# A fused attention and MLP kernel: seven block products for eight in the last blocks of the first MLP product, one more batch turned by DMA, new priorities

## The chip, the core and the metric

The kernel runs on one core of a Trainium2 chip. The metric is the device time in microseconds (us) of one execution; three executions of the kernel before took 311.2, 312.96 and 313.85 us, and their median, **312.96 us**, is the time before. Besides that one execution was profiled; its span from the first to the last instruction is 311.4 us, and all times "at" which something happens are counted from the start of that span.

TensorE (PE in the profile) multiplies matrices into PSUM, a memory of eight banks of 512 fp32 columns for each of 128 partitions. ScalarE (ACT), VectorE (DVE) and GpSimd (POOL) work on tiles; SyncE (SP) issues transfers. Each engine takes its own instructions strictly in order and waits on semaphores for the others.

## What is computed

The reference, cut to what matters:

```python
# 8 batches, 8 heads, 576 tokens, 64 per head; omega: 128 x 64
scale = 1.0 / np.sqrt(np.sqrt(D))
def phi(x):                                   # x = q*scale or k*scale
    proj = np.einsum('bhsd,md->bhsm', x, omega)
    sq = np.sum(x * x, axis=-1, keepdims=True) / 2.0
    h = proj - sq
    h = h - np.max(h, axis=-1, keepdims=True)
    return np.exp(h) / np.sqrt(m)
q_p, k_p = phi(q_s), phi(k_s)
kv = np.einsum('bhsm,bhsd->bhmd', k_p, v)
z = np.sum(k_p, axis=2)
num = np.einsum('bhsm,bhmd->bhsd', q_p, kv)
den = np.einsum('bhsm,bhm->bhs', q_p, z)[..., None] + 1e-06
attn = num / den
x = attn.transpose(0, 2, 1, 3).reshape(4608, 512)
h = x @ w_in                                  # first MLP product, 512 -> 2048
g = h * np.clip(h + 3.0, 0.0, 6.0) / 6.0
out = g @ w_out                               # second MLP product, 2048 -> 512
```

So a linear attention over features gives x (4608 tokens of 512), and a two-layer MLP with the hard-swish function follows.

## The kernel before

The kernel is written as a list of operations with what each reads and writes, its possible engines, its expected duration and a priority. A list scheduler in the kernel's own Python code (class Prog) sorts these into one fixed order for each engine, gives PSUM banks to the operations' results ("Virt" is a bank that is asked for), and puts in the semaphore waits. A table NUDGE shifts single priorities and changes nothing but the order.

The tokens are worked on in nine blocks of 512: blocks 0 to 7 are the first 512 tokens of each batch, block 8 the 64 left over of each batch. While TensorE does the MLP of one block it also does the attention of a later batch, so matmuls of several kinds lie between each other. The first MLP product of a block is made by feature columns, 16 groups of 128:

```python
    def mm1(blk, f):
        ...
        def e(E):
            for c in range(NJ):                                  # NJ = 4 pieces of the 512 inputs
                ins = E.matmul(ring.t[vh.slot], wi[:, c, 128 * f:128 * f + 128], xv[:, c, :],
                               start=(c == 0), stop=(c == NJ - 1))
            return ins
        op("PE", 4 * mmt(512), e, t, ..., name="mm1.%d.%d" % (blk, f))            # L998
        op("ACT", ..., lambda E: E.activation(tsb[tu][:], ring.t[vh.slot], AF.Relu,
                                              bias=0.5, scale=1.0 / 6.0), ...)     # L1004
        op("DVE", ..., lambda E: E.scalar_tensor_tensor(gT[gu][:, f, :], tsb[tu][:], 1.0,
                                              ring.t[vh.slot], ALU.min, ALU.mult), ...)  # L1006
```

The second MLP product (L1132) already goes by seven products of quarters in place of eight from block 1 on. GpSimd makes the sums of quarters of g that it needs (L1064); VectorE adds its parts (L1148). Block 0's first and second product are at L1023 and L1048, the very last product at L1198.

```python
    def products(blk):
        h0, ha, hb = Virt(ring), Virt(ring), Virt(ring)          # three PSUM banks
        plan = [(h0, 0, block(blk, 0, 0), B11, ...), (h0, 0, block(blk, 0, 1), B21, ...),
                (ha, 0, S2[gu], T2, ...), (ha, 0, S3[gu], B12, ...), (hb, 0, block(blk, 1, 0), T1, ...),
                (ha, 0, block(blk, 1, 1), T4, ...), (hb, 0, block(blk, 0, 1), B22, ...)]
        # each: 16 matmuls of 256 columns
```

Attention turns q, k and its own output x by 128 x 128 pieces. The first three batches (0 to 2) are turned on TensorE (L511) with a copy out of PSUM behind it; from the fourth batch on a transposing DMA does it:

```python
    PE_T, PE_X = 3, 3          # batches below this number: q/k and x turned on TensorE
        ...
        if b < PE_X:
            turn_x(0, 4, [0, 1])
        else:
            op("SP", 0.9, lambda E: E.dma_start_transpose(
                xT[pb][:, m, :].rearrange("p (t k) -> p t k", t=4), xm[pb][:, m, :]), ...)   # L974
```

From the fourth batch on (ROWS = 3) the projections of k and q come in "bursts" of matmuls over 64 rows, two at a time on the two halves of the array (L736 and L739). k and q of successive batches land in two buffers in turn (one of them is the memory of the fp32 staging of batch 0), and so does x:

```python
    half = k32[:].rearrange("p c d -> p (c d)").bitcast(BF16)
    KB = [kb, half[:, 0:NCH * D]...]                  # k of even / odd batches
    QB = [qb, half[:, NCH * D:2 * NCH * D]...]
    xb = [sbt("xb%d" % u, [128, XW], BF16) for u in range(2)]
```

Before the first inputs have landed, TensorE is given filler matmuls (L548) that compute nothing of use.

Of the kernel before, what the change touches and what calls it, by code (L numbers as in the profile page):

```python
# [15 lines left out]
ROWS = 3  # L16
# [6 lines left out]
    ('Tevk0.00', 0): 0.0222, ('Tk0.10', 0): 0.0169, ('Tevk0.10', 0): 0.0216, ('Tk0.11', 0): 0.0313,  # L23
    ('Tevk0.11', 0): 0.0172, ('castq0.0A', 0): -0.0176, ('Tevq0.1A', 0): 0.1639, ('Tq0.1B', 0): -0.0037,
    ('Tevq0.1B', 0): 0.3021, ('Tk0.l', 0): 0.4022, ('Tevk0.l', 0): 0.0235, ('K0.0', 0): -0.1553,
    ('eK0.0', 0): -0.0153, ('K0.1', 0): 0.0442, ('eK0.1', 0): -0.0653, ('mx0.1', 0): -0.0395, ('eK0.2', 0): -0.042,
    ('K0.3', 0): 0.0766, ('K0.4', 0): 0.1229, ('eK0.4', 0): 0.2718, ('K0.5', 0): -0.0067, ('eK0.5', 0): 0.0177,
    ('K0.6', 0): -0.0736, ('eK0.6', 0): 0.1839, ('mx0.6', 0): 0.3237, ('K0.7', 0): -0.0092, ('eK0.7', 0): 0.8775,
    ('K0.8', 0): 0.0351, ('eK0.8', 0): 0.0218, ('mx0.8', 0): -0.0031, ('eQ0.0A', 1): 0.7881, ('vcl.0', 1): 0.0286,
    ('cc.0.0', 0): 0.1338, ('kvz.0.0', 0): 0.1537, ('num.0.0A', 0): 0.0042, ('rec.0.0A', 0): -0.0049,  # L30
    ('div.0.0A', 0): 0.0356, ('num.0.0B', 0): 0.0126, ('vc.0.1', 0): 0.4124, ('kv.0.1', 0): -0.0134,
    ('kvz.0.1', 0): 0.8635, ('num.0.1A', 0): 0.0126, ('rec.0.1A', 0): -0.009, ('div.0.1A', 0): 0.177,
    ('Xev.0.1A', 0): 0.6709, ('num.0.1B', 0): -0.0007, ('cc.0.2', 0): -0.0088, ('vc.0.2', 0): 0.1154,
    ('vcc.0.2', 0): -0.0808, ('num.0.2A', 0): 0.0126, ('rec.0.2A', 0): 0.08, ('vc.0.3', 0): -0.0114,
    ('vcc.0.3', 0): -0.0172, ('num.0.3A', 0): 0.7836, ('X.0.3B', 0): 0.0821, ('Xev.0.3B', 0): 0.0062,
    ('numL0', 0): -0.0033, ('divL0', 0): 0.0082, ('divL2', 0): 0.0082, ('k00.1', 0): 0.0095, ('kl.1', 0): -0.0088,
    ('ql0.1', 0): 0.0145, ('vl.1', 0): -0.119, ('v10.1', 0): -0.0099, ('Tevq1.2', 0): 0.0463, ('Tq1.4', 0): 0.7514,
    ('mx1.4', 0): -0.179, ('eK1.5', 0): 0.3592, ('mx1.5', 0): 0.3227, ('eK1.6', 0): 0.7632, ('mx1.7', 0): -0.561,
    ('mx1.8', 0): 0.0033, ('Q1.0', 1): 0.0073, ('eQ1.0', 1): 1.061, ('Q1.1', 0): 0.0184, ('Q1.1', 1): -0.0218,
    ('eQ1.1', 1): 0.9399, ('Q1.2', 1): 0.3729, ('eQ1.2', 1): -0.007, ('Q1.3', 0): 1.0729, ('vcl.1', 1): -0.0035,  # L40
    ('cc.1.0', 0): -0.1361, ('vc.1.0', 0): 0.0089, ('kv.1.0', 0): 0.0071, ('kvz.1.0', 0): -0.0003,
    ('rec.1.0A', 0): 0.0024, ('div.1.0A', 0): 0.0054, ('div.1.0B', 0): 0.0054, ('vc.1.1', 0): 0.0087,
    ('num.1.1A', 0): -0.002, ('div.1.1A', 0): 0.0054, ('div.1.1B', 0): 0.0054, ('Xev.1.1', 0): -0.0002,
    ('kv.1.2', 0): 0.9899, ('rec.1.2A', 0): -0.0101, ('div.1.2A', 0): 0.0075, ('div.1.2B', 0): 0.0054,
    ('X.1.2', 0): 0.0047, ('vc.1.3', 0): 0.6341, ('rec.1.3A', 0): -0.0016, ('div.1.3A', 0): 0.0054,
    ('div.1.3B', 0): 0.0054, ('mm1.0A.0p', 2): 0.0169, ('mm1.0A.2p', 1): 0.003, ('mm1.0A.2p', 2): 0.026,
    ('mm1.0A.4p', 2): 0.0282, ('mm1.0A.4', 0): 0.0113, ('relu.0A.4', 0): 0.1116, ('mm1.0A.6', 0): -0.0758,
    ('relu.0A.6', 0): -0.0575, ('mm1.0A.8', 0): -0.0075, ('g.0A.8', 0): -0.037, ('g.0A.10', 0): 0.0321,
    ('relu.0A.12', 0): 0.0317, ('mm1.0A.14', 0): 0.0222, ('relu.0B.12', 0): 0.7429, ('relu.0B.14', 0): 0.6881,
    ('k10.2', 0): -0.0002, ('kl.2', 0): -0.7114, ('q10.2', 0): 0.511, ('ql0.2', 0): 0.6465, ('Tevq2.3', 0): -0.6541,  # L50
    ('Tq2.4', 0): 1.2316, ('K2.2', 0): -0.7584, ('K2.5', 0): -0.3285, ('mx2.5', 0): -0.1483, ('K2.6', 0): 0.784,
    ('K2.7', 0): -0.0504, ('K2.8', 0): -0.1148, ('mm2.0.0', 3): -0.0049, ('mm2.0.0', 5): 1.9062,
    ('mm2.0.0', 6): 0.0051, ('mm2.0.1', 2): 0.0111, ('mm2.0.1', 5): 0.4836, ('mm2.0.2', 0): -0.0003,
    ('mm1.1.0', 0): -1.129, ('mm1.1.8', 0): -1.8251, ('g.1.8', 0): 0.0106, ('mm1.1.1', 0): -1.2275,
    ('mm1.1.9', 0): -0.9344, ('relu.1.9', 0): 0.0261, ('mm1.1.2', 0): -0.5674, ('mm1.1.10', 0): -1.3861,
    ('mm1.1.11', 0): -0.0435, ('mm1.1.4', 0): -0.3428, ('mm1.1.12', 0): 0.0488, ('mm1.1.13', 0): -0.1387,
    ('relu.1.13', 0): -0.4107, ('mm1.1.14', 0): 0.8048, ('mm1.1.7', 0): 0.8803, ('relu.1.7', 0): 0.0128,
    ('g.1.7', 0): -0.0389, ('mm1.1.15', 0): 1.161, ('k10.3', 0): -0.0369, ('kl.3', 0): 0.0052, ('q00.3', 0): -0.0024,
    ('q10.3', 0): 0.0694, ('ql0.3', 0): -0.0408, ('ql1.3', 0): -0.013, ('eK3.3.0', 0): 1.4387, ('R3.4', 0): -0.4628,
    ('eQ3.4', 0): -0.8607, ('kv.3.1', 0): 1.0065, ('vcc.3.2', 0): -0.4962, ('kv.3.2', 0): 0.1102,  # L60
    ('cc.3.3', 0): -0.8518, ('kvz.3.3', 0): 0.0243, ('P1.2', 0): 0.9757, ('P1.4', 0): 0.3487, ('P1.5', 1): -0.0512,
    ('P1.6', 1): 0.5369, ('mm1.2.0', 0): -1.4622, ('mm1.2.8', 0): -1.4018, ('mm1.2.1', 0): -1.442,
    ('g.2.1', 0): -0.019, ('mm1.2.9', 0): -0.3004, ('mm1.2.2', 0): -0.8136, ('mm1.2.11', 0): 0.359,
    ('mm1.2.12', 0): 0.5284, ('mm1.2.5', 0): 0.5493, ('mm1.2.6', 0): 0.5785, ('mm1.2.14', 0): 0.4337,
    ('mm1.2.7', 0): 0.6223, ('mm1.2.15', 0): 0.272, ('kl.4', 0): 1.3248, ('q00.4', 0): 3.3283, ('R4.4', 0): 1.7005,
    ('kv.4.1', 0): 1.244, ('kv.4.2', 0): 2.3155, ('rec.4.2B', 0): -0.9675, ('rec.4.3B', 0): -2.0089,
    ('P2.0', 0): 0.8372, ('mm1.3.2', 0): 0.2569, ('mm1.3.3', 0): 1.5479, ('mm1.3.4', 0): 1.276,
    ('mm1.3.5', 0): 1.2524, ('mm1.3.13', 0): 1.3245, ('mm1.3.6', 0): 1.4395, ('relu.3.6', 0): -0.4435,
    ('mm1.3.14', 0): 1.2483, ('mm1.3.7', 0): 1.5772, ('relu.3.7', 0): -0.3792, ('mm1.3.15', 0): 2.2545,
    ('kl.5', 0): 1.5071, ('q00.5', 0): -1.2639, ('eQ5.1', 0): -0.7262, ('eK5.2.0', 0): -1.0927,  # L70
    ('eK5.2.1', 0): -0.7425, ('eQ5.2', 0): -0.2778, ('eQ5.2', 1): -1.2134, ('eK5.3.0', 0): -1.1241,
    ('eQ5.3', 0): -0.7781, ('eQ5.3', 1): -1.1002, ('rec.5.0B', 0): 0.3333, ('num.5.1A', 0): 0.9799,
    ('vc.5.2', 0): -0.2083, ('div.5.2A', 0): 1.0671, ('P3.0', 0): 1.894, ('p1.3', 0): -2.2681,
    ('mm1.4.8', 0): -0.5145, ('mm1.4.1', 0): -1.527, ('S24.0', 0): 0.3404, ('relu.4.10', 0): -0.4615,
    ('mm1.4.11', 0): 0.2614, ('g.4.11', 0): 1.1488, ('S24.3', 0): -0.7607, ('eK6.0.0', 0): 1.1035,
    ('R6.1', 0): -0.8985, ('eQ6.1', 0): 1.5979, ('vc.6.0', 0): -1.609, ('vcc.6.0', 0): -1.6609, ('kv.6.0', 0): 0.7643,
    ('S44.1', 0): -1.9992, ('P4.2', 1): -0.8623, ('P4.3', 1): -2.077, ('P4.4', 1): -1.4771, ('mm1.5.0', 0): -1.6247,
    ('mm1.5.8', 0): -0.9391, ('mm1.5.1', 0): -1.9248, ('S35.0', 0): 0.1833, ('mm1.5.2', 0): -1.0023,
    ('relu.5.2', 0): 1.3127, ('mm1.5.11', 0): -1.1438, ('mm1.5.6', 0): 0.544, ('mm1.5.14', 0): 0.9483,
    ('mm1.5.7', 0): 0.6794, ('k00.7', 0): -0.8986, ('k10.7', 0): -1.1588, ('kl.7', 0): -0.7342, ('q10.7', 0): -0.2825,  # L80
    ('ql0.7', 0): -1.5109, ('ql1.7', 0): -1.5993, ('R7.1', 0): -1.3631, ('eQ7.1', 1): -0.9517, ('R7.4', 0): -0.7767,
    ('kv.7.0', 0): -0.5374, ('num.7.0A', 0): -0.5449, ('div.7.2B', 0): 1.8188, ('kv.7.3', 0): 0.8011,
    ('kvz.7.3', 0): 2.1121, ('num.7.3A', 0): 0.8703, ('P5.0', 0): 0.8394, ('P5.4', 0): 0.6698,
    ('mm1.6.0', 0): -0.9734, ('mm1.6.8', 0): -0.5602, ('mm1.6.1', 0): -0.5771, ('mm1.6.9', 0): -0.2962,
    ('mm1.6.2', 0): -0.4166, ('mm1.6.10', 0): -0.1926, ('mm1.6.3', 0): -0.3888, ('mm1.6.11', 0): 0.3862,
    ('mm1.6.12', 0): 0.4482, ('mm1.6.13', 0): 0.606, ('mm1.6.6', 0): 0.5263, ('mm1.6.14', 0): 0.7093,
    ('mm1.6.15', 0): 0.6324, ('P6.0', 0): 0.8219, ('P6.2', 0): 0.2249, ('P6.2', 1): -0.859, ('P6.4', 0): 0.6817,
    ('P6.6', 0): -0.9586, ('P6.6', 1): -1.2152, ('mm1.7.7', 0): -1.7654, ('P7.5', 1): 0.9958, ('P7.6', 1): 0.9926,
# [1225 lines left out]
```

The softmax here doesn't subtract the row's maximum and nothing guards it: scores larger than these inputs give would overflow.

## Time and profile before

| | |
|---|---|
| time, median of three | 312.96 us |
| span of the profiled execution | 311.4 us |
| TensorE busy | 301.0 us (97%) |
| VectorE busy | 231.9 us (74%) |
| GpSimd busy | 230.2 us (74%) |
| ScalarE busy | 195.5 us (63%) |
| moved by DMA | 43.17 MB, mean 139 GB/s |

How to read it. A page of the profile gives for each engine the time in which it was busy and its share of the span, then the same in 40 equal slices as tenths. PEld is the loading of weights into the array, which overlaps the matmuls. The "chain that ended last" is followed back from the last instruction, at each step to what released it. A "group" is all instructions of one line, engine and operation: busy time and mean duration of one in ns, then the idle time of the engine just before them and what ended it. Matmul durations contain their passage through the array and so overlap; the pace of a row of matmuls is its length divided by their number. The same holds, to a lesser degree, of the other engines. The other views used are the busy time by stretch, the timeline, and the chain in order of time (start, length, engine and line, number).

### The profile page before, as it was taken

The page shows a single profiled execution, that of the slowest core. Times are in us where ns is not written, and L with a number is a line of the kernel's source. Part 1 is how long each engine was busy: PE and PEld are TensorE (multiplying, and loading weights), DVE is VectorE, ACT ScalarE, POOL GpSimd, SP SyncE. Part 2 cuts the span into 40 slices and gives each one's busy share as a digit, 9 for nine tenths or more (in the row PEclk, how much of TensorE's full clock was granted, in tenths as well). Part 3 has the DMA queues.
Part 4 walks back from the last instruction along what each step waited for, and adds up shares of the span by engine and source line. Part 5 has one row for each costly group of instructions (what it writes and reads, how often), then busy time and mean ns, then how long its engine had stood idle before and what let it go on. Part 6 is the DMA issues. An engine that isn't in the chain of part 4 may idle for free.

```text
span 311.4 us, 7144 instructions
## 1 busy us (share of the span) xinstructions
PE 301.0 (97%) x2723; PEld 204.4 (66%) x2750; DVE 231.9 (74%) x511; ACT 195.5 (63%) x448; POOL 230.2 (74%) x246
## 2 busy tenths in 40 slices
PE   7999999999999999999999999998999999999993
PEld 5679966555775578656864685467745864567783
DVE  4898998797778965879687977975978627558543
ACT  3786898598658763878389836992867106455200
POOL 2687454299989797499959995999759936839990
PEclk9999999999999999999999999999999999999999
DMA  7999999997747899389959992999511201010036
GB/s 240 254 205 182 249 180 161 255 113 100 158 131 98 96 251 221 141 111 153 252 129 168 199 179 85 127 188 213 133 78 37 42 10 61 2 67 0 2 135 137
DMA packets 83218, 43.17 MB, mean 139 GB/s; under 512 B 51056, under 2 KB 80880, under 8 KB 83184
## 3 DMA queue, kind: packets, MB, share of 16 engines
q1 hardware_dynamic: 55824, 29.60, 40.4%
q0 software_dynamic: 26576, 12.46, 32.3%
q10 hardware_dynamic: 784, 0.66, 0.7%
q8 instruction: 22, 0.36, 0.5%
q14 instruction: 12, 0.10, 0.1%
HBM read 36.73 MB, written 9.44 MB: 148 GB/s over the span
## 4 chain that ended last, share of the span: by engine, by line
PE 80%; POOL 8%; ACT 3%; DMA 2%; issue 2%; DVE 2%; SPq 1%; POOLq 0%; DVEq 0%
PE p L998 30%; PE p L1132 27%; PE p L1048 5%; PE p L1023 4%; POOL s L1064 4%; PE p L929 2%; DMA q<-in_q_dram 2%; PE p L511 2%; PE p L900 2%; PE p L736 2%; POOL gT L1064 1%; POOL vc L884 1%; PE p L739 1%; PE p L771 1%; PE p L788 1%
## 5 line engine op out<-in xcount | busy, mean ns | idle before, releaser
L1006 DVE SCALAR_TENSOR_TENSOR gT<-tsb,p 128x512 f16<-128x512 f16 x128 | 84.9, 681 | 28.4 <-ACT tsb L1004 27.7
L1004 ACT ACTIVATE tsb<-p 128x512 f16<-128x512 f32 x128 | 74.8, 600 | 45.1 <-PE p L998 36.7
L998 PE MATMUL p<-xT,wi 128*128 128x512 bf16 x427 | 101.2, 379 | 1.5 <-issue 0.3
L998 PEld LDWEIGHTS p<-xT,wi 128*128 128x128 bf16 x448 | 42.2, 98 | 44.0 <-issue 1.1
L1132 PE MATMUL p<-wo,gT 128*128 128x256 f16 x368 | 45.7, 273 | 0.0
L1064 POOL TENSOR_TENSOR s<-gT 128x512 f16<-128x512 f16 x32 | 37.0, 1156 | 11.8 <-DVE gT L1006 9.8
L1064 POOL TENSOR_TENSOR s<-gT,s 128x512 f16<-128x512 f16 x32 | 37.0, 1156 | 8.8 <-DVE gT L1006 6.7
L1064 POOL TENSOR_TENSOR gT<-gT,s 128x512 f16<-128x512 f16 x32 | 36.9, 1153 | 5.7 <-PE p L1132 3.4
L1132 PEld LDWEIGHTS p<-wo,gT 128*128 128x128 f16 x368 | 35.0, 98 | 6.8 <-issue 0.8
L1064 POOL TENSOR_TENSOR gT<-gT 128x512 f16<-128x512 f16 x32 | 37.4, 1167 | 2.4
L749 ACT ACTIVATE kp<-p 128x512 bf16<-128x512 f32 (+1 forms) x50 | 25.8, 560 | 19.4 <-PE p L739 19.3
L754 DVE TENSOR_REDUCE mx<-kp 128x4 f32<-128x512 bf16 (+1 forms) x50 | 29.6, 625 | 4.5 <-ACT kp L749 4.0
L1132 PE MATMUL p<-t,gT 128*128 128x256 f16 x256 | 32.1, 273 | 0.0
L945 DVE TENSOR_TENSOR xb<-p,rec 128x384 bf16<-128x384 f32 (+1 forms) x64 | 28.5, 476 | 0.2
L884 POOL TENSOR_TENSOR vc<-v,cc 128x512 bf16<-128x512 f32 x22 | 23.4, 1062 | 6.9 <-DVE cc L878 4.9
L758 ACT ACTIVATE qpT<-p 128x512 bf16<-128x512 f32 (+1 forms) x50 | 26.5, 576 | 2.2 <-PE p L739 2.2
L1132 PEld LDWEIGHTS p<-t,gT 128*128 128x128 f16 x256 | 24.2, 98 | 5.6 <-issue 1.2
L1148 DVE TENSOR_TENSOR u<-p 128x512 f32<-128x512 f32 x16 | 11.0, 690 | 13.4 <-PE p L1132 13.4
L780 DVE TENSOR_REDUCE mx<-kp 128x4 f32<-128x512 bf16 x27 | 17.5, 675 | 1.2 <-ACT kp L777 1.2
L886 ACT ACTIVATE vc<-v,cc 128x64 bf16<-128x64 f32 x72 | 18.2, 351 | 0.0
L811 POOL TENSOR_TENSOR vcl<-vl,cc 64x260 bf16<-64x260 f32 x14 | 8.7, 620 | 11.8 <-DVE cc L807 11.0
L929 PEld LDWEIGHTS p<-kvz,qpT 128*128 128x128 bf16 x312 | 14.2, 98 | 4.9 <-ACT qpT L792 0.5
(101 smaller groups left out, 474.6 us busy)
## 6 DMA issues: line engine op xcount, KB each, us to landing
v<-in_v_dram SPq DMA_DIRECT2D x14, 512.0 KB, 5.1
out_dram<-osb SPq DMA_DIRECT2D x14, 512.0 KB, 2.7
wi<-in_moe_w_in_dram POOLq DMA_DIRECT2D x4, 512.0 KB, 9.0
k<-in_k_dram POOLq DMA_DIRECT2D x8, 256.0 KB, 4.6
k<-in_q_dram POOLq DMA_DIRECT2D x8, 256.0 KB, 5.3
wo<-in_moe_w_out_dram POOLq DMA_DIRECT2D x8, 256.0 KB, 12.3
kb<-in_k_dram POOLq DMA_DIRECT2D x6, 256.0 KB, 5.1
qb<-in_q_dram POOLq DMA_DIRECT2D x6, 256.0 KB, 5.2
```

The lines of the kernel that those rows point to most:

```text
L749: op("ACT", actt(128 * n), lambda E, lh=lh, ko=ko: E.activation(ko, out_of(0, lh).rearrange("p (x m) -> p x m", m=M), AF.Exp, scale=alpha) ...
L754: op("DVE", dvet(128 * n), lambda E, ko=ko, mo=mo: E.reduce_max(mo, ko, axis=AX.X), pos(u) + 0.03, reads=[("kp", 0, u + lh) if i else ("kp ...
L758: op("ACT", actt(128 * n), lambda E, lh=lh: E.activation(qd[:, d0:d1, lh, :], out_of(1, lh).rearrange("m (j t) -> m j t", t=128), AF.Exp, ...
L884: return E.tensor_tensor(vcm[:, :, 0:D], v32[:, m, :, :], cbc, ALU.mult)
L886: ins = E.activation(vcm[:, i, 0:D], v32[:, m, i, :], AF.Copy, scale=cc[pb][:, c0 + i:c0 + i + 1])
L929: ins = E.matmul(d[:, hh, i - i0, :], qpT[pb][:, o:o + 128], kvz[m][:, 65 * hh:65 * hh + 65], start=True, stop=True)
L945: op("DVE", dvet(128 * n), lambda E: E.tensor_tensor(xv(i0, i1), psum()[:, :, :, 0:64], rbc, ALU.mult), t + 0.01, reads=[vn, ("rec", ru)], ...
L998: ins = E.matmul(ring.t[vh.slot], wi[:, c, 128 * f:128 * f + 128], xv[:, c, :], start=(c == 0), stop=(c == NJ - 1))
L1004: op("ACT", actt(512), lambda E: E.activation(tsb[tu][:], ring.t[vh.slot], AF.Relu, bias=0.5, scale=1.0 / 6.0), t - 0.1, reads=[vh], write ...
L1006: op("DVE", dvet(512), lambda E: E.scalar_tensor_tensor(gT[gu][:, f, :], tsb[tu][:], 1.0, ring.t[vh.slot], ALU.min, ALU.mult), t - 0.1, re ...
L1064: op(engines, {"POOL": 0.05 + n / 490.0, "DVE": 0.07 + n / 1920.0}, lambda E: E.tensor_tensor(dst, x, y, ALU.subtract if minus else ALU.ad ...
L1132: ins = E.matmul(ring.t[v.slot][:, 256 * j:256 * j + 256], a[:, f, 128 * j:128 * j + 128], w[:, f, :], start=(first and f == 0 and j == 0) ...
```

## The change: what it does and what it is for

1. **Seven products for eight in the first MLP product**, for the second half of block 7's feature groups and all of block 8. A pair of feature groups (f and f + 8) and the two halves of the tokens and of the inputs make 2 x 2 quarters. Sums of quarters of w_in (input_sums, once, on VectorE) and of x (x_sums, for both blocks, on VectorE or GpSimd) take the place of some quarters. Seven products of quarters, each of two matmuls of 256 columns, replace eight. The parts are put together in PSUM: TensorE adds to a bank, ScalarE copies from bank to bank, VectorE adds. It is meant to take matmul time away.

2. **Third batch's output turned by transfers**: PE_X goes from 3 to 2, so batch 2's x is turned by DMA rather than on TensorE.

3. **Types and buffers.** x and w_in are held in f16 in place of bf16. The memory of the fp32 staging of batch 0 now holds the sums, so that k and q have one buffer for all batches, and so has x.

4. **Bursts.** Their code is rewritten, with a list of ranges (BURSTS) of the same five ranges; it applies from the same batch on. Their order among the rest comes from other priorities, and the batches from the fifth on have a shorter step (APACE).

5. **Priorities**: a new NUDGE table, and another expected duration of GpSimd's sums in the scheduler.

The diff, cut to its core (cuts marked with ...):

```diff
 NUDGE = {
-    ('Tevk0.00', 0): 0.0222, ...
+    ('k00.0', 0): -0.0886, ...
@@
+    ROWS = 3
+    BURSTS = [[(0, 2)], [(2, 6)], [(6, 10)], [(10, 14)], [(14, 18)]]
+    FAST = 4
+    APACE = 0.06
-    PE_T, PE_X = 3, 3
+    PE_T, PE_X = 3, 2
@@
-    half = k32[:].rearrange("p c d -> p (c d)").bitcast(BF16)
-    KB = [kb, half[:, 0:NCH * D]...]
-    QB = [qb, half[:, NCH * D:2 * NCH * D]...]
+    stage = [t[:].rearrange("p c d -> p (c d)").bitcast(F16) for t in (k32, q32)]
+    W2s, W3s = [stage[0][:, 2048 * i:2048 * i + 2048]... for i in range(2)]
+    W4s = stage[1][:, 0:2048]...
+    X1s, X2s, X4s = ...                       # further parts of stage
-    xb = [sbt("xb%d" % u, [128, XW], BF16) for u in range(2)]
-    xT = [sbt("xT%d" % u, [128, NJ, MAIN], BF16) for u in range(2)]
-    wi = sbt("wi", [128, NJ, DFF], BF16)
+    xb = [sbt("xb", [128, XW], F16)] * 2
+    p7 = [sbt("p7_%d" % u, [128, 256], F32) for u in range(2)]
+    X3s = [sbt("x3_%d" % u, [128, 2, 256], F16) for u in range(2)]
+    xT = [sbt("xT%d" % u, [128, NJ, MAIN], F16) for u in range(2)]
+    wi = sbt("wi", [128, NJ, DFF], F16)
@@
+    FIRST7 = (8, 7)          # first block of feature groups 0-3 and 4-7
+    AHEAD = 2                # a pair starts when the pair two before has ended
+    def input_sums(h):       # W1..W4 of 128x1024 each, on VectorE
+        ...
+    def x_sums(blk):         # X1..X4 of 128x512 each, on VectorE or GpSimd
+        ...
+    def mm1_pair(blk, f):
+        U, V = Virt(ring, True), Virt(ring, True, True)          # two PSUM banks
+        ...
+        def e_a(E):
+            two(E, half(U, 0), orig(0, 0), b[0][0], True)        # two matmuls of 256 columns
+            return two(E, half(U, 1), summed(W3s), X3s[u])
+        def e_b(E):
+            two(E, half(V, 1), summed(W2s), X2s[u])
+            return two(E, half(U, 0), orig(0, 1), b[1][0])
+        def e_d(E):
+            two(E, half(V, 1), orig(1, 1), X4s[u])
+            return two(E, half(V, 0), summed(W4s), b[1][1])
+        op("PE", 2 * each, e_a, ..., name="mm1a." + nm)
+        op("ACT", actt(256), lambda E: E.copy(half(V, 1), half(U, 0)), ..., name="s1." + nm)
+        op("ACT", actt(256), lambda E: E.copy(p7[w7][:], half(U, 1)), ..., name="s3." + nm)
+        op("PE", 2 * each, e_b, ..., name="mm1b." + nm)
+        op("ACT", actt(256), lambda E: E.copy(half(V, 0), half(V, 1)), ..., name="s2." + nm)
+        op("PE", each, lambda E: two(E, half(V, 0), summed(wi[:, 0:2, 1024:2048]), X1s[u]), ..., name="mm1c." + nm)
+        op("DVE", dvet(256), lambda E: E.tensor_tensor(half(U, 1), half(V, 0), p7[w7][:], ALU.add), ..., name="a2." + nm)
+        op("DVE", dvet(256), lambda E: E.tensor_tensor(half(V, 1), half(V, 1), p7[w7][:], ALU.add), ..., name="a1." + nm)
+        op("PE", 2 * each, e_d, ..., name="mm1d." + nm)
+        # then Relu on ScalarE and min-and-multiply on VectorE for U and V, 512 columns each, as before
@@
-        op(engines, {"POOL": 0.05 + n / 490.0, ...
+        op(engines, {"POOL": 0.07 + n / 455.0, ...
```

In the pair the order is fixed by what each piece reads: a, then the copies s1 and s3, then b, then the copy s2, then c, then the additions a2 and a1, then d.

## The prediction

> **What bounds the kernel now.** I read the page first (shares of engines, the slices), then the chain that ended last, then busy time by stretch, then the groups. The page:
>
> ```profile
> PE 301.0 (97%) x2723; PEld 204.4 (66%) x2750; DVE 231.9 (74%) x511; ACT 195.5 (63%) x448; POOL 230.2 (74%) x246
> PE   7999999999999999999999999998999999999993
> PEclk9999999999999999999999999999999999999999
> PE 80%; POOL 8%; ACT 3%; DMA 2%; issue 2%; DVE 2%; SPq 1%; POOLq 0%; DVEq 0%
> ```
>
> TensorE (PE) is busy in every slice but the first and the last, at the full clock, and 80% of the chain that ended last is its own. The stretches say where the rest is:
>
> ```profile
> core 0: us, PE busy (x) PEld busy (x) DVE busy (x) ACT busy (x) POOL busy (x), PEclk, DMA share, GB/s
> 0.00:22.00 22.00, 19.31 (x200) 13.62 (x201) 15.53 (x51) 14.50 (x32) 11.90 (x22) 1.00 1.00 235
> 191.00:225.00 34.00, 33.00 (x315) 21.64 (x317) 26.09 (x60) 25.57 (x64) 29.57 (x32) 1.00 0.85 158
> 253.00:276.00 23.00, 22.89 (x130) 12.72 (x130) 14.11 (x21) 11.34 (x20) 11.87 (x11) 1.00 0.12 47
> 276.00:292.00 16.00, 15.90 (x112) 10.98 (x113) 10.07 (x17) 7.80 (x14) 13.66 (x13) 1.00 0.01 1
> 292.00:311.40 19.40, 14.52 (x141) 12.80 (x138) 8.19 (x14) 0.33 (x1) 11.34 (x10) 0.96 0.38 109
> ```
>
> From 22 us to 306 us TensorE hardly pauses: even the worst stretch, 191 to 225, lacks 1.0 us. In the last two blocks (253 to 292) it lacks 0.2 us of 39. Up to 22 us the program waits for its first inputs, and part of PE's busy time there is filler (59 matmuls at L548). So past the start the time is TensorE's work laid end to end, and a change is worth the matmul time that it takes away, less the waits that it brings in. From the chain in order of time I take the pace of each kind:
>
> ```profile
> 39.83 0.67 PE p L511 x12
> 280.30 2.59 PE p L998 x12
> 291.59 13.17 PE p L1132 x120
> ```
>
> A 128-column transpose costs 0.67/12 = 0.056 us, a 512-column matmul of the first product 2.59/12 = 0.216 us, a 256-column one 13.17/120 = 0.110 us. The mean durations in the groups (379 and 273 ns) are longer because they overlap. Two 256-column matmuls cost 0.22 us, the same as one of 512, so cutting the product into quarters costs nothing by itself.
>
> **What the Trainium skill says.** "TensorE: Matmul & The Clock Gate", section "Back-to-back issue gap", gives an isolated gap of N/2.4 + 2.5 ns when warm: 216 ns for 512 columns, 109 for 256, 56 for 128. The trace agrees with all three; the 131 ns that the same section gives for sustained streams of 512 is not seen here. "VectorE: DVE Perf Modes", section "Why PSUM operands drop a tier", says that fp32 PSUM operands hold VectorE to its 1x mode; the trace agrees, 681 to 692 ns for 512 elements, so each added 256-column addition in PSUM will be near the 416 ns of the 128x256 group below. "DMA: Bandwidth & Descriptors", section "DMA Transpose (X-bar)", says that a transposing DMA takes 2-byte types only; xb goes from bf16 to f16, which is still 2 bytes, so the transfers should keep their median landing time of 4.0 us.
>
> **The change part by part.**
>
> ```profile
> L1006 DVE SCALAR_TENSOR_TENSOR gT<-tsb,p 128x512 f16<-128x512 f16 x128 | 84.9, 681 | 28.4 <-ACT tsb L1004 27.7
> L1004 ACT ACTIVATE tsb<-p 128x512 f16<-128x512 f32 x128 | 74.8, 600 | 45.1 <-PE p L998 36.7
> L499 ACT COPY xT<-p 128x256 bf16<-128x256 bf16 x5 | 1.8, 374 | 0.9 <-PE p L511 0.9
> L865 DVE TENSOR_TENSOR xb<-p,rec 128x256 bf16<-128x256 f32 x2 | 0.8, 416 | 0.0
> L511 PE MATMUL p<-ident,xb 128*128 128x128 bf16 x48 | 5.3, 219 | 0.1
> ```
>
> *Seven products for eight.* Half of block 7 and all of block 8, 24 of the 144 feature columns of 128, go over to pairs: 12 pairs. A pair took 8 matmuls of 512 columns, 8 x 0.216 = 1.73 us; it now takes 14 of 256, 14 x 0.1095 = 1.53 us. The instruction orders of both programs agree: 512 matmuls of 512 columns become 416, and 168 of 256 columns come in. TensorE saves 96 x 0.216 - 168 x 0.1095 = 20.7 - 18.4 = **2.3 us**, all in the stretch where it had no idle time.
>
> What it costs elsewhere: per pair three ScalarE copies of 128x256 (374 ns each in the group above) and two VectorE additions of 128x256 (416 ns). Over 12 pairs ScalarE gets 36 x 0.374 = 13.5 us more and VectorE 24 x 0.416 = 10.0 us more. In 253 to 292 they had 11.34 + 7.80 = 19.1 us and 14.11 + 10.07 = 24.2 us of 39. ScalarE goes to 32.6 us, VectorE to 34.2 us, plus six of the eight sums of x quarters on it (some 0.35 us each, estimated from half of the 0.67 us that a 1024-element f16 sum took: 2.1 us), 36.3 us in all. The stretch itself shrinks to 36.7. That looks full, but durations count overlap: where operations follow each other without a wait, VectorE starts a 512-element one every 0.60 us, not 0.69 (3 in 2.05 us at 274 us in the timeline), and ScalarE one every 0.48. By pace VectorE has some 31 of 36.7. The eight weight sums (8 x some 0.7 = 5.6 us of VectorE) lie mostly (six of the eight, by the order) before block 7's pairs, where VectorE had 20.1 of the 28 us from 225 to 253.
>
> *The round trips.* Inside a pair TensorE waits three times for another engine. After a group comes the drain, 273 - 109 = 0.16 us, and some 0.03 us of signalling (ScalarE ends at 256.70, VectorE starts at 256.73). So: a 0.44, out 0.19, copy 0.40, b 0.44, out 0.19, copy 0.40, c 0.22, out 0.19, two additions 0.77, d 0.44: a chain of 3.7 us for 1.53 us of TensorE. Alone it would stall more than half of the time. But the new order puts 208 matmuls of the second product (22.8 us) between the pieces, and lets two pairs run at once: TensorE has (18.4 + 22.8)/12 = 3.4 us of work per pair, 6.9 us for two, against a chain of 3.7. So most pieces find their operand waiting. Where two copies or a Relu stand ahead of the one needed, a piece is late by a few tenths. I put **0.7 us** for all 12 pairs; this is a choice.
>
> *Third batch's output by transfers.* The 48 transposes of xb become 32; 16 x 0.056 = **0.9 us** off TensorE, and the copies out of PSUM with them (four of 512 columns). Four more DMA transposes at 4.0 us land well ahead: in that stretch the second block's products run and DMA is not full.
>
> *Buffers.* The batches' k and q now land in one pair of buffers instead of two (the old second pair holds the sums), and xb is single. A load must wait until the previous batch has been turned. A batch has some 32 us; landing takes 5 us and the turns 4 us each. **0** expected.
>
> *Priorities and bursts.* The same 180 + 50 matmuls of the bursts; five vc scalings move from GpSimd to ScalarE. TensorE idles so little between 22 and 292 that better priorities can give back about 1 us at most. In the start, 60 filler matmuls for 59 say that the scheduler expects the same empty time. I take **-0.3 us**.
>
> Sum: 312.96 - 2.3 - 0.9 + 0.7 - 0.3 = 310.2. As the list of priorities was made for this order, and such lists are kept where they help, I go a little lower: **309.8 us**, 1.0% less.
>
> **The rivals.** (1) *The round trips eat the gain.* Engines take their work in order, so one late copy delays the matmuls behind it, those of the second product too. For it: three waits per pair, ScalarE and VectorE both near nine tenths by duration, and two PSUM banks held per pair beside three of the second product, of eight. Against it: 6.9 us of work over a 3.7 us chain. At 0.3 us per wait, 36 waits are 10.8 us and the change would be slower, near 320; at 0.1 us they are 3.6 and the change is worth nothing. (2) *VectorE becomes the bound of the last two blocks*: if it really takes 0.69 us for each operation, 36.3 us of 36.7 leaves no room and some 2 us are lost: 311.5. (3) *The single buffers delay a batch*: a burst late by 2 us is covered as long as other matmuls are ready; only if the block before had run out would it cost, 1 to 3 us. (4) *The priorities do more than I see*, above all in the first 22 us: with an earlier first product 2 us less, 307.8.
>
> **Range and chances.** The three runs before span 311.2 to 313.85, so the measure alone wanders by a per cent. Sums of the good cases (no late pieces, 1 us from priorities, 1 us from the start) give 307.5; of the bad (rivals 1 and 2 at 0.1 us a wait) 313. Range 306.8 to 312.8. Faster by over 2% means under 306.7, which needs rival 4 whole and nothing lost: 0.09. Slower by over 2% means over 319.2, rival 1 in full: 0.03. Within 2%: 0.88.
>
> **What the profile after will show.** If right: TensorE's matmul time down by 3.2 us; PE still near nine tenths or more in every slice from the third to the last but one; in the last two blocks, waits of PE for ScalarE copies and VectorE additions that sum to under 1.5 us; VectorE and ScalarE at 80 to 90% there; first product at L1023's successor starting near 21.5 us as before. The saving is wrong if 256-column matmuls at odd weights run slower than 0.1095 us; the 0.7 is wrong if the pieces of pairs show gaps of 0.2 us or more each; the buffers are wrong if TensorE idles between 92 and 253 us by clearly more than the 2.3 us of 161 that it lacks there now by the same view of stretches. Wrong altogether if the last stretch grows rather than shrinks.

## The result, and the profile after

The changed kernel takes **308.59 us** (median of six executions, 308.26 to 310.21), the kernel before beside it 311.92 us (six, 310.85 to 313.85): a ratio of 0.9896, with a 95% interval of 0.9856 to 0.9936. The profiled execution of the kernel after spans 306.5 us. Its page, first the shares of the engines, then two rows of slices and the shares of the chain that ended last:

```profile
PE 298.6 (97%) x2804; PEld 210.0 (69%) x2807; DVE 246.1 (80%) x543; ACT 215.4 (70%) x522; POOL 229.9 (75%) x248
...
PE   8999999999999999999999999999999899999994
...
PE 88%; DVE 4%; ACT 3%; DMA 2%; SPq 2%; issue 1%; DVEq 0%
```

TensorE is still busy throughout, and its part of the chain grew from 80% to 88%. GpSimd left the chain, in which it had 8%; VectorE has 4% where it had 2%. The busy time by stretch of the kernel after, cut where its blocks 7 and 8 lie (start:end, length, busy time of PE, PEld, DVE, ACT, POOL):

```profile
0.00:22.00 22.00, 20.19 (x220) 15.44 (x221) 16.05 (x54) 15.44 (x35) 13.33 (x23) 1.00 1.06 247
...
225.00:241.20 16.20, 14.97 (x118) 7.96 (x114) 15.71 (x33) 7.48 (x16) 8.00 (x7) 1.00 0.29 70
241.20:253.00 11.80, 11.80 (x85) 8.15 (x86) 10.17 (x20) 8.32 (x19) 10.50 (x9) 1.00 0.01 1
253.00:276.00 23.00, 23.00 (x204) 19.56 (x202) 18.49 (x34) 14.67 (x34) 21.05 (x19) 1.00 0.12 47
276.00:289.00 13.00, 13.00 (x122) 11.63 (x120) 11.45 (x22) 8.29 (x19) 12.11 (x11) 1.00 0.01 2
```

From 241.2 to 289 us, where the twelve pairs lie but for the first piece of the first one (at 239.4 us), this view shows no idle time of TensorE: the round trips cost nothing that it can see. The one lack is just ahead of them, 1.2 us between 225 and 241.2, and there VectorE is full (15.71 of 16.2). The list of TensorE's waits in the kernel after, from 18 us on (who waits, for whom, us in all, times, longest), has only two entries:

```profile
PE p L1037 <- DVE gT L1045: 1.2, 1, 1.2
PE p L1037 <- ACT qpT L832: 0.5, 1, 0.5
```

What VectorE did ahead of the first is told by its chain in order of time (start, length, engine and line):

```profile
232.83 0.81 DVE xb L984 x2
234.15 0.68 DVE gT L1045
234.83 1.34 DVE q L1222
236.17 0.87 DVE gT L1045 x2
237.28 1.50 DVE wi L1222
238.78 1.30 DVE q L1222
240.53 0.61 DVE gT L1045
241.19 2.77 PE p L1037 x12
```

L1222 are the sums of quarters of x and w_in. They stand in VectorE's order ahead of the g (L1045) that frees a PSUM bank for TensorE's next group, and three of them last 1.3 to 1.5 us, where the prediction had 0.35 us for a sum of x quarters and 0.7 us for one of w_in. The timeline of the kernel after shows why:

```profile
234.73 1.16 POOL L1222 TENSOR_TENSOR s<-gT 128x512 f16<-128x512 f16 x1
234.75 1.42 DVE L1222 TENSOR_TENSOR q<-xT 128x512 f16<-128x512 f16 x1
...
238.33 1.46 POOL L1222 TENSOR_TENSOR q<-xS 128x512 f16<-128x512 f16 x1
238.71 1.37 DVE L1222 TENSOR_TENSOR q<-xT,q 128x512 f16<-128x512 f16 x1
240.11 0.42 DVE L1222 TENSOR_TENSOR k<-xT,q 128x512 f16<-128x512 f16 x1
```

A VectorE sum of this size takes 0.42 us alone (the last line) and 1.42 us beside a sum on GpSimd that started 0.02 us earlier. It ends at 236.17, 0.28 us after GpSimd's ends at 235.89. The Trainium skill, "SBUF — State Buffer", section "Who interferes with whom", says it: a VectorE instruction with two SBUF inputs contends with a GpSimd instruction that reads SBUF, for a pair of ports that one of the two holds exclusively, and the order of issue decides which of them waits. The prediction did not draw on it. This trace agrees in the lengths (0.42 against 1.37 to 1.42 us). Who goes first can't be read from starts so close together: at 243.18 us another VectorE sum starts 0.02 us behind GpSimd's as well, and there it takes 0.42 us and GpSimd's 1.45. So the cost differs between executions of one program: in the profile of e0_after below, TensorE waits twice behind such sums, 2.1 us in all.

### The profile page after: what moved, and what is told of

It is laid out like the page before. It is cut to its first block, busy times and chain, and to the rows that moved or that the text cites. A ratio compares the mean times of both kernels' runs of the same rounds, so it can differ in the third digit from the quotient of the medians.

```text
span 306.5 us, 7393 instructions
## 1 busy us (share of the span) xinstructions
PE 298.6 (97%) x2804; PEld 210.0 (69%) x2807; DVE 246.1 (80%) x543; ACT 215.4 (70%) x522; POOL 229.9 (75%) x248
## 4 chain that ended last, share of the span: by engine, by line
PE 88%; DVE 4%; ACT 3%; DMA 2%; SPq 2%; issue 1%; DVEq 0%
PE p L1290 31%; PE p L1037 27%; PE p L1116 6%; PE p L1181 4%; PE p L1206 4%; PE p L968 3%; PE p L940 3%; PE p L764 2%; DMA v<-in_v_dram 2%; PE p L767 2%; PE p L828 2%; ACT kp L815 1%; SPq L619 1%; PE p L541 1%; DVE gT L1045 1%; DVE q L1222 1%
## 5 line engine op out<-in xcount | busy, mean ns | idle before, releaser
L1037 PE MATMUL p<-xT,wi 128*128 128x512 f16 x416 | 97.4, 380 | 1.8 <-DVE gT L1045 1.2
L1045 DVE SCALAR_TENSOR_TENSOR gT<-tsb,p 128x512 f16<-128x512 f16 x104 | 68.0, 681 | 14.3 <-ACT tsb L1043 13.7
L1043 ACT ACTIVATE tsb<-p 128x512 f16<-128x512 f32 x104 | 59.7, 601 | 20.4 <-PE p L1037 17.2
L1037 PEld LDWEIGHTS p<-xT,wi 128*128 128x128 f16 x416 | 38.9, 98 | 42.6 <-DVE gT L1045 1.8
L1222 POOL TENSOR_TENSOR s<-gT 128x512 f16<-128x512 f16 x32 | 37.1, 1160 | 13.7 <-DVE gT L1045 10.1
L1222 POOL TENSOR_TENSOR s<-gT,s 128x512 f16<-128x512 f16 x32 | 37.5, 1173 | 6.5 <-DVE gT L1045 4.6
L1222 POOL TENSOR_TENSOR gT<-gT,s 128x512 f16<-128x512 f16 x32 | 36.9, 1154 | 3.6 <-PE p L1290 1.1
L1222 POOL TENSOR_TENSOR gT<-gT 128x512 f16<-128x512 f16 x32 | 37.2, 1163 | 2.4
L783 ACT ACTIVATE kp<-p 128x512 bf16<-128x512 f32 (+1 forms) x50 | 25.9, 559 | 8.8 <-PE p L767 8.7
L984 DVE TENSOR_TENSOR xb<-p,rec 128x384 f16<-128x384 f32 (+1 forms) x64 | 28.8, 474 | 0.2
L926 ACT ACTIVATE vc<-v,cc 128x64 bf16<-128x64 f32 x112 | 28.4, 363 | 0.0
L924 POOL TENSOR_TENSOR vc<-v,cc 128x512 bf16<-128x512 f32 x17 | 18.4, 1080 | 8.9 <-DVE cc L918 7.7
L619 POOL DMA_DIRECT2D kb<-in_k_dram x21 | 16.2, 782 | 8.3 <-PE p L1037 4.8
L619 POOL DMA_DIRECT2D qb<-in_q_dram x28 | 19.5, 710 | 1.7 <-PE p L968 0.8
L1163 ACT ACTIVATE tsb<-p 128x512 f16<-128x512 f32 x24 | 14.3, 598 | 8.1 <-PE p L1116 5.2
L968 PEld LDWEIGHTS p<-kvz,qpT 128*128 128x128 bf16 x312 | 15.0, 98 | 5.0 <-issue 0.2
```

Of the source, the lines that this page charges most:

```text
L619: lambda E: E.dma_start(dst, src), prio + 0.001 * turn_of[0], reads=gate, writes=keys,
L783: op("ACT", actt(128 * (d1 - d0)), lambda E, lh=lh, ko=ko, part=part: E.activation(ko, out_of(part, 0, lh)[0].rearrange("p (x m) -> p x m" ...
L926: ins = E.activation(vcm[:, i, 0:D], v32[:, m, i, :], AF.Copy, scale=cc[pb][:, c0 + i:c0 + i + 1])
L968: ins = E.matmul(d[:, hh, i - i0, :], qpT[pb][:, o:o + 128], kvz[m][:, 65 * hh:65 * hh + 65], start=True, stop=True)
L984: op("DVE", dvet(128 * n), lambda E: E.tensor_tensor(xv(i0, i1), psum()[:, :, :, 0:64], rbc, ALU.mult), t + 0.01, reads=[vn, ("rec", ru)], ...
L1043: op("ACT", actt(512), lambda E: E.activation(tsb[tu][:], ring.t[vh.slot], AF.Relu, bias=0.5, scale=1.0 / 6.0), t - 0.1, reads=[vh], write ...
```

## The experiments

The theory after reading the trace: the products gave their 2.3 us of matmul time, the round trips took nothing, and some 1.2 us was lost in VectorE's locked sums; the transfers gave 0.9 us; the priorities gave little. The rivals: the new order of the instructions is itself the gain, or the start is. In the tables below, "idle" is TensorE's time from one matmul's start to the next beyond the pace of its size (216, 109 and 56 ns for 512, 256 and 128 columns), counted from 18 us on. Some 4.5 us of it are alike in every row: the 48 changes between the 64-row matmuls of the bursts and matmuls of the full array, 0.09 us each. What counts is the difference between rows.

### Parts undone, and the order made anew

First the changed kernel again (e0_after), beside three versions in which one setting was changed and the scheduler made a new order:

> The changed kernel once more, to be compared on the same chip with the three below. Expected 308.6 us as on record, 0.990 of before (0.986 to 0.994).

```diff
-    FIRST7 = (8, 7)          # e1_no7: no pairs; blocks 7 and 8 by eight products,
+    FIRST7 = (9, 9)          #         with the old priorities for them
```

> The changed kernel with eight products everywhere (no pairs, no sums of quarters of x and w_in), with the old priorities for blocks 7 and 8. My theory (TensorE's work laid end to end): 2.3 us of matmul time come back, and the one wait of 1.2 us that TensorE has at 240 us, behind VectorE's sums of x, goes: 309.7, 1.1 us more than the changed kernel; its trace should show no PE idle time over 0.3 us between 222 and 290 us. Rival (the priorities carry the gain, the round trips eat what the products save): 308.6 or less.

```diff
-    PE_T, PE_X = 3, 2        # e2_x3
+    PE_T, PE_X = 3, 3
```

> The changed kernel with the third batch's output turned on TensorE again (16 transposes more). My theory: 16 x 0.056 = 0.9 us more on TensorE, 309.5 us. Rival (the transfer form has its own waits, or the transposes filled gaps): the same 308.6 within 0.3.

```diff
-    XADD = ("DVE", "POOL")   # e3_xpool: the eight sums of x quarters on GpSimd alone
+    XADD = ("POOL",)
```

> The changed kernel with all eight sums of x quarters on GpSimd, none on VectorE. Theory: two of VectorE's sums of x and one of w_in took 1.4 to 1.5 us in place of 0.42 and 0.68 where a GpSimd sum was running, and this made the wait of 1.2 us at 240 us; with the sums on GpSimd the wait goes and the time falls by about 1 us, to 307.6. Rival (the wait is only VectorE's own load, or GpSimd's 1.16 us per sum, three of them in a chain, make the pairs' first pieces late): the same or up to 1 us more.

| version | us, median | ratio to before, 95% interval | expected |
|---|---|---|---|
| e0_after | 309.06 | 0.9901 [0.9866, 0.9936] | as the result |
| e1_no7 | 323.93 | 1.0385 [1.0344, 1.0426] | 309.7 |
| e2_x3 | 310.34 | 0.9945 [0.9917, 0.9972] | 309.5 |
| e3_xpool | 326.08 | 1.0442 [1.0400, 1.0484] | 307.6 |

e2 is 1.3 us above e0, where 0.9 was expected; e11 below comes back to it. e1 and e3 miss by 14 and 18 us. Neither says what the part is worth. The list of TensorE's waits in e3 begins:

```profile
PE p L1290 <- POOL s L1222: 3.5, 2, 1.8
PE p L1116 <- DVE p L1154: 3.1, 4, 1.5
PE p L1116 <- POOL q L1222: 2.6, 1, 2.6
```

A few operations fewer or elsewhere, and the scheduler with the tuned priorities made another order. In e1 the sums of w_in, six of which stand in VectorE's order from 27 us on in the kernel after, are gone, and TensorE's list has 3.3 us of waits between 92 and 126 us, where the kernel after has none, far from the pairs that were taken out. In e3 the pairs (L1116) stand where their inputs are late; 7.5 us of its list are waits for GpSimd's sums, so a part of its loss may be the eight sums themselves, as the rival said. The two are not separated here. The priorities were tuned for one list of operations. So from here on the scheduler is replaced by a record: every operation keeps its place on its engine and its PSUM bank from the kernel after, and one thing is edited in the record.

```diff
     def schedule(self):
-        ...                                          # list scheduling by priorities
+        for name, k, eng, slots, end, after in ORDER:   # as recorded from the kernel after
+            o = at[(name, k)] = by.pop((name, k))
+            o.eng = eng
+            for d in after:                          # extra waits (none in the record itself)
+                o.deps[at[d]] = True
+            ...                                      # banks as recorded
```

### Parts undone within the same order

e4_after is the kernel after itself, from which the record is taken. The record unedited was not run; e7 below, which adds nothing but waits to it, has the same instructions in the same order as e4 on all four engines. In e5 the 12 pairs become 24 groups of four 512-column matmuls at the places of their pieces a and d; copies, additions and sums are left out. e6 also turns the third batch's x on TensorE, 16 transposes at the place of the transfers; e11 does only this.

> The changed kernel as the baseline of the three below, on their chip: 0.990 of before, as in its two earlier comparisons.

> The changed kernel's own recorded order of every engine, kept instruction by instruction, with one thing done to it: each pair becomes two groups of four 512-column matmuls again (at the places of the pair's first and last pieces, in its two banks), and the copies, additions and sums of quarters are dropped. My theory: 2.3 us of matmul time come back and the wait of 1.2 us behind VectorE's sums goes: 1.1 us more than the changed kernel, PE idle under 0.3 us from 222 to 290 us. Rival (the round trips eat what the products save): the same time or less. If the loss of 15 us of the version without pairs that was scheduled anew were due to the missing pairs, it would show here too; if it was due to the new order, it won't.

> As the last, and the third batch's output is turned on TensorE again (16 transposes, put in where their operands are ready): the old kernel's work in the new kernel's order, buffers and types. Theory: 0.9 us more than the last one, 2.0 us more than the changed kernel. What then is left against the kernel before is the share of order, priorities and buffers: by my sum 1 us or so less than before (ratio near 0.996). Rival (the priorities carry the gain): as fast as the changed kernel.

> The changed kernel's recorded order, with the third batch's output turned on TensorE again (16 transposes, put in where their operands are ready). By the count 0.9 us more; the same step cost 3.0 us between the two versions without pairs, of which their traces show 0.9 in transposes, 0.5 in waits around them and 1.4 us at the start, before anything of this change. If the start is chance, this one is 0.9 to 1.5 us above the changed kernel, 309.8 to 310.3; if turning on TensorE costs more by itself, 311 and above.

```diff
 # e5, e6: the record, for each pair
-mm1a.8.0  s1.8.0  s3.8.0  mm1b.8.0  s2.8.0  mm1c.8.0  a2.8.0  a1.8.0  mm1d.8.0
+mm1.8.0                                                               mm1.8.8
-W1 W2 W3 W4, X1.7 ... X4.8
 # e6, e11: the record, for each quarter m of batch 2
-Xdma.2.m (SP)
+X.2.m (PE), Xev.2.m (DVE)
```

| version | us, median (lowest) | ratio to before, 95% interval | over e4 | idle from 18 us | of it at 230 to 241.5 |
|---|---|---|---|---|---|
| e4_after | 308.77 (308.28) | 0.9910 [0.9875, 0.9945] | | 6.97 | 1.16 |
| e5_no7_same_order | 309.67 (309.34) | 0.9943 [0.9924, 0.9962] | +0.9 | 5.68 | 0.00 |
| e6_old_work_same_order | 312.63 (311.32) | 1.0034 [1.0017, 1.0052] | +3.9 | 6.55 | 0.00 |
| e11_x3_same_order | 309.96 (309.56) | 0.9947 [0.9931, 0.9963] | +1.2 | 7.57 | 0.00 |

e8 to e11 ran on another chip than e4 to e7, with the kernel before at 311.85 us beside them against 311.62; the ratios allow for that.

e5 lands where it was expected (+1.1): the seven products are worth about 1 us, 2.3 us of matmul time less a stall of 1.2 us. In e5's trace that stall is gone; one wait of TensorE is left from 18 us on:

```profile
PE p L1026 <- ACT qpT L821: 0.5, 1, 0.5
```

e11 lands where it was expected too (309.8 to 310.3): the transfers are worth 0.9 us of transposes and some tenths of waits around them. (One of its 22 executions took 389 us, at a granted clock of 0.755; the median does not feel it.) In e11 the stall ahead of the pairs sits a little later, 1.0 of the 1.18 us that it idles in 241.5 to 292; the order of the rest is the same.

e6 was expected near 0.996 and came to 1.0034. Its matmul time is 3.2 us above e4's and its idle time 0.4 us below, which makes 2.8. The shortest spans from the first to the last instruction differ by just that (309.3 against 306.5 us), the medians of the spans by 3.5 and the medians of the times by 3.9. So the missing 1 us does not lie in the order past the start. 0.4 of it lies outside the span: the time exceeds the span by 2.15 us in the median of e6's executions, by 1.8 in that of e4's and of the kernel before's, and why is open. The rest differs from execution to execution, as the start does, which is shown next. What e6 does say: with the old amount of work the new order, made for the new work and patched here, is no faster than the kernel before, so order, priorities, buffers and the rewritten bursts together show no gain of their own.

### The start

The first product of block 0 ended at 39.56 us in the profile before and at 36.96 in the profile after, 2.6 us apart, nearly all of the gain if it lasted. So the kernel before was profiled once more:

> The kernel before, for a second profile. In the first one its first product of block 0 ended at 39.56 us, in the changed kernel at 37.0 us, with 6.8 and 4.6 us of empty time on TensorE up to there and the k and q loads landing 1 to 2 us later in the kernel before. If the new priorities of the start make the difference, this profile has it again: 39.6 us within 0.3. If it is the landing of the first loads, which varies from run to run, it can be anything from 37.5 to 39.6 here.

It ended at 37.78 us there (one time, 312.11 us). And versions that are alike up to there differ as much among themselves: 37.08 us in e4, 37.30 in e7, 39.34 in e8. The useful matmuls up to that point come to 26.3 us before and 25.9 after, so what varies is the empty time, 5.1 to 6.8 us in the two profiles before and 4.6 to 6.9 in those of the versions after. In the first profile before, the last two of k's five pieces landed at 7.4 and 8.4 us, in the profile after at 6.1 and 6.6. The landing of q's fourth large piece accounts for the end of that product to within 0.1 us. In both profiles before, the product ends 28.1 us after it (it lands at 11.44 and at 9.66 us). In the versions after, it ends 27.3 us after it where the piece lands by 10.05 us (eight profiles, e4 and e7 among them) and 28.2 us after it where it lands from 10.19 to 11.09 us (four, e6 and e8 among them). **The start wanders by up to 2.4 us from one execution to the next.** At the same landing (9.66 us in the second profile before, 9.67 in the profile after) the new start ends 0.8 us earlier, and half of that is matmul work which it leaves for later (26.3 against 25.9 us); after a late landing it gains nothing. So the change has at most some tenths in it. A single pair of profiles would have credited the change with all of it.

### The locked sums

In e7 five GpSimd sums wait for the VectorE sum beside which they ran; nothing else is moved. T3 is a sum of quarters of w_out. In e8 eight do, so that every sum of x, the first of W1 and T3 run alone.

```diff
 # e7: the record, extra waits (operation: after)
+S36.1 (POOL): X1.7 (DVE)
+X3.7  (POOL): W1   (DVE)
+X1.8  (POOL): X2.7 (DVE)
+S27.0 (POOL): W1, second half (DVE)
+S31.2 (POOL): T3, second half (DVE)
 # e8: other pairs for the x sums, so that all of them are apart
+X3.7  (POOL): X4.7 (DVE)
+X1.8  (POOL): X3.8 (DVE)
+S26.1, S36.3 (POOL): X2.8 (DVE)
+S16.1 (POOL): X4.8 (DVE)
```

> The changed kernel's recorded order, with five GpSimd sums made to wait for the VectorE sum beside which they ran (the sum of block 6 for X1, X3 for W1, X1 of block 8 for X2, one of block 7 for the second W1, one of block 1 for T3). Theory (a VectorE sum of two f16 tiles in SBUF stands still while a GpSimd sum runs, and the other way round): these VectorE sums take 0.42 and 0.68 us in place of 1.4 to 1.8, TensorE's waits of 1.2 us at 240 us and part of the 0.6 us at 78 us go: 1.2 to 1.8 us less than the changed kernel. Rival (the sums are slow for another reason, as their inputs landing, or TensorE waits for something else there): the same time, and VectorE's sums as long as before.

> As the version with GpSimd's sums kept apart from VectorE's, but now for all of the eight sums of x: there the clash had only moved on to X4 of block 7 and X2 of block 8 (1.26 and 1.40 us), with TensorE's wait of 0.9 us behind them. Now X3 waits for X4, X1 of block 8 for X3 of block 8, and two sums of block 6 for X2 of block 8. Theory: VectorE's sums of x at 0.42 us each, the wait goes, 0.9 us less than the last version: 306.5 us, ratio near 0.984. Rival (GpSimd's sums now come too late for the pairs' first piece or for the second product of block 6): no gain, with TensorE waiting for GpSimd at 239 to 247 us.

| version | us, median (lowest) | ratio to before, 95% interval | over e4 | idle from 18 us | 230 to 241.5 | 241.5 to 292 |
|---|---|---|---|---|---|---|
| e7_ports_apart | 307.44 (307.17) | 0.9870 [0.9835, 0.9905] | -1.3 | 5.95 | 0.15 | 1.01 |
| e8_ports_apart_all | 307.34 (306.97) | 0.9859 [0.9832, 0.9885] | -1.4 | 5.69 | 0.38 | 0.54 |

The timeline of e7, where the sum that took 1.42 us runs alone:

```profile
234.33 0.42 DVE L1221 TENSOR_TENSOR q<-xT 128x512 f16<-128x512 f16 x1
234.67 1.28 DVE L1044 SCALAR_TENSOR_TENSOR gT<-tsb,p 128x512 f16<-128x512 f16 x2
234.83 1.16 POOL L1221 TENSOR_TENSOR s<-gT 128x512 f16<-128x512 f16 x1 [0.60 <-DVE q L1221]
236.56 0.69 DVE L1221 TENSOR_TENSOR wi<-wi 128x1024 f16<-128x1024 f16 x1 [0.61 <-PE p L1036]
...
237.62 1.26 DVE L1221 TENSOR_TENSOR k<-xT,q 128x512 f16<-128x512 f16 x1
...
241.53 1.40 DVE L1221 TENSOR_TENSOR q<-xS,q 128x512 f16<-128x512 f16 x1
```

0.42 us for 1.42, 0.69 for 1.50; GpSimd lost 0.6 us of waiting that nobody misses. The second line is the control: two g with one operand in PSUM and one in SBUF run beside GpSimd's sum at their usual 0.6 us each. The last two lines show the clash come back at later sums (1.26 and 1.40 us), and TensorE's wait with it, behind the second of them, at 243.6 us:

```profile
PE p L1036 <- DVE gT L1044: 0.9, 1, 0.9
```

The other entry of the kernel after's list, 0.5 us put down to ScalarE (qpT) at 78 us, is gone from e7's list too: T3 takes 0.69 us there for 1.76, and it is the only edited sum before 92 us. With the other x sums apart as well (e8) all x sums on VectorE take 0.42 or 0.43 us, but now TensorE waits for GpSimd's delayed sums, in the second product (L1295) and in a pair (L1121), as the rival said:

```profile
PE p L1295 <- POOL s L1227: 0.4, 1, 0.4
PE p L1121 <- POOL x L1227: 0.2, 1, 0.2
```

So e7's -1.3 us is what was expected (-1.2 to -1.8), and e8's further 0.1 us (0.3 by the ratios), less than its spread, is not (306.5 was expected). **e8 is the fastest version**, 1.4% under the kernel before and about 0.5% under the kernel after (307.34 against 308.77 us in e4). Its interval overlaps that of e4; that the waits help rests on four things together: the medians of both versions, the durations, the idle time, which fell by 1.0 and 1.3 us, and the single executions, of which nine of the twelve of e7 and e8 are shorter than the shortest of the eighteen of the kernel after (308.16 us).

### Pairs without cover

In e10 four pairs of block 8 (1, 3, 5, 7) have their pieces one behind the other on TensorE; what lay between follows them.

```diff
 # the record, for pairs 8.1, 8.3, 8.5, 8.7
-mm1a ... mm1b ... mm1c ... mm1d        (... = matmuls of other products)
+mm1a mm1b mm1c mm1d ...
```

> The changed kernel's recorded order, but in four of the twelve pairs (1, 3, 5 and 7 of block 8) nothing of another kind lies between the pair's first and last piece on any engine: the pieces that did stand after the pair. By the prediction's sum a pair's chain is 3.7 us for 1.53 us of matmuls, so TensorE should wait 2.1 us in each of the four: 8.6 us more than the changed kernel, less what a neighbour's pieces gain by it: 315 to 317 us. Rival (the copies and additions cost TensorE nothing because they are short): under 311.

It took 321.7 us (1.0323 [1.0288, 1.0358]), above what was expected. TensorE idles 10.8 us after 250 us, 2.7 per pair, which the list of its waits divides among the three round trips:

```profile
PE p L1121 <- DVE p L1159: 4.0, 4, 1.0
PE p L1121 <- ACT p L1151: 3.0, 4, 0.7
PE p L1121 <- ACT p L1154: 1.8, 4, 0.4
```

Four waits of each, 8.8 us in all, 2.2 per pair; the rest, 0.5, is the 0.16 us by which a matmul's duration exceeds its pace, three times. One bare pair ran from 265.29 to 269.52 us: a chain of 4.2 us for 1.53 us of TensorE. Of the prediction's 3.7 us, most of the lack is one step: piece b waits for both copies s1 and s3 (copies start at 265.93 and 266.20, b at 266.63), not for one. (The spans of the two profiled executions, 319.5 and 306.5 us, differ by these 10.8 us and by 2.2 for e10's late start, 39.26 against 37.08 us. That the medians differ by 12.9 as well, though the start varies, is left open.) All twelve pairs bare would thus cost some 12 x 2.7 = 32 us, an estimate. In the kernel after, where other products lie between, 0.15 us of idle time are left from 241.5 to 292 us.

## Why the prediction held, step by step

The result, 308.59 us, lies within the range and 1.2 us under the predicted 309.8. Most of this is the base: the kernel before took 312.96 us in the three executions that the prediction started from and 311.92 in the six beside the result. The predicted gain was 3.2 us, the measured one 3.3. The sum behind it is not what happened, though: gains that did not come and costs that did not come met, and that they met is luck.

- **Matmul time, -2.3 us: right.** 416 matmuls of 512 columns are left (the group below), and 256-column ones at the new weights run at 109 ns, f16 like bf16.
- **Round trips, +0.7 us: mis-sized.** 0.15 us of idle time from 241.5 to 292 in the kernel after (1.1 in e0, 0.9 of it a wait behind a locked sum). The mechanism (two pairs at once, the second product between) was right, and e10 shows what it hides: the chain is 4.2 us and not 3.7, and 6.9 us of work for two pairs covers it all the same.
- **The sums on VectorE: the step that failed.** "Some 0.35 us each" was half of what a 1024-element sum took, measured alone. They took 0.42 us alone and up to 1.42 beside GpSimd, and came in a row of three just where a g was due. That cost 1.2 us at 240 us. Another 0.6 us went at 78 us behind T3 (1.76 us), by the idle time of e4 and e7 up to 92 us, 1.23 and 0.58. The kernel before had this sum too; there it started 0.1 us ahead of GpSimd's and took 0.68 us. Six of the eight sums of w_in ran from 27 to 55 us, not in the stretch from 225 to 253 us where the prediction counted VectorE's room, and took 0.68 us each. The prediction counted the sums as load of an engine with room; as a wait in front of a needed operation they had no entry in the sum.
- **Transfers, -0.9 us: right**, and a few tenths more (e11, 1.2 us). **Buffers, 0: right** as far as seen: TensorE is busy throughout from 92 to 225 us. In the first profile before, 27 matmul records are missing, and part of the 2.3 us that the prediction read there may never have been; the second, with none missing, lacks 1.0 us from 92 to 253 us, 0.8 of it in one wait for a GpSimd sum, which is gone in the kernel after.
- **Priorities, -0.3 us, and "a little lower": not shown.** e6 leaves nothing for them: that wait for a GpSimd sum is gone there too, but in all e6 idles only 0.3 us less than the second profile before (6.55 against 6.9). The argument that such lists are kept where they help holds for the whole change; it says nothing of the gain. Its part may rather be to keep the change from losing, as e1 suggests.
- **Rivals.** 1 (round trips eat the gain) falls. 2 (VectorE becomes the bound) came true for 8 us ahead of the pairs and not in the last blocks: there VectorE had 40.1 of 47.8 us (84%), ScalarE 31.3 (65%, where 80 to 90% was said). 3 (buffers) was not seen. 4 (the start) fooled the first reading: the first product began at 17.6 us, not "near 21.5 us as before". Some 1.8 us of that is chance: it began at 19.8 us in the second profile before, at the same landing as after. The rest is the new order, but by the end of that product only 0.8 us of it is left.

The groups of the kernel after that answer to those of before:

```profile
L1037 PE MATMUL p<-xT,wi 128*128 128x512 f16 x416 | 97.4, 380 | 1.8 <-DVE gT L1045 1.2
L1045 DVE SCALAR_TENSOR_TENSOR gT<-tsb,p 128x512 f16<-128x512 f16 x104 | 68.0, 681 | 14.3 <-ACT tsb L1043 13.7
```

Means and paces are those of before; only the counts fell. By the times, products are worth 2.3 - 1.2 = about 1 us and transfers about 1.2 (e5 and e11, +0.9 and +1.2), which leaves about 1 of the 3.3 us. The traces say what it is. The second profile of the kernel before has 3.2 us more of matmul time than e4 and, past 18 us, the same idle time (6.9 against 7.0 us). What the changed kernel loses ahead of the pairs (1.2 us) it gains for the most part at this wait of the kernel before, at 215 us, which the lists of the kernel after and of e4 to e7 and e11 do not have:

```profile
PE p L1132 <- POOL s L1064: 0.8, 1, 0.8
```

So the gain is the matmul time of both parts, 2.3 + 0.9 us. The spans of these two profiles differ by 3.8 us (310.3 and 306.5); most of the rest is empty time of the start (5.1 against 4.7 us). Which edit took the old wait away was not tested; e6 lacks it as well, so it was neither the products nor the transfers.

## What to carry to other kernels

Where one engine is the bound and work is laid end to end on it, cut that engine's time and fill each round trip with other work of the same engine: 4.2 us chains for 1.5 us of matmuls vanished here. When new work goes to a side engine, ask not only whether it has room, but what stands right behind it in its order, and whether a neighbour shares its port. And to learn what a part of a scheduled kernel is worth, freeze the order and edit it: in e1 the order made anew cost 14 us, much of it in waits far from the part.

## What the runs showed of the hardware

- A VectorE sum of two SBUF tiles and a GpSimd sum exclude each other. Behind GpSimd a VectorE sum of 512 elements takes up to 1.42 us for 0.42 and ends 0.28 us after GpSimd's; one of 1024 takes up to 1.76 for 0.69 and ends 0.55 us after it. A GpSimd sum of 512 takes up to 1.48 us for 1.16 in the kernel after (1.70 in e0, 1.60 in the kernel before) when VectorE's came first, and ends 1.01 us after VectorE's. Starts 0.03 us apart do not tell which comes first: T3 starts 0.03 us ahead of GpSimd's sum (72.91 and 72.94 us) and is the one that waits. Operations with only one SBUF input were untouched (0.68 us).
- A round trip from TensorE over ScalarE or VectorE and back, through PSUM, with nothing between, cost 0.9 us of idle time on average (2.7 us for three).
- A change between matmuls of 64 rows and of the full array cost 0.09 us beyond the pace, each way (48 changes in e4).
- The landing of the first inputs moved the start by up to 2.4 us between executions of like programs: q's fourth large piece landed at 9.67 us in the profile after and at 11.09 in e8.
